# Letting the list scheduler choose between VectorE and GpSimd for SBUF-to-SBUF work, with a longer allowance for loads

## The chip, the cores and the metric

The kernel runs on one core of a Trainium2 chip. The metric is the device time of one execution in microseconds, the median of several runs. TensorE (PE) multiplies, VectorE (DVE), ScalarE (ACT) and GpSimd (POOL) do the elementwise work, and SyncE's queue (SP) issues nearly all DMAs.

## The reference

Three blocks follow each other. Windowed attention makes 1152 token rows of 512. A mixture of four experts (each 512 to 1024 to 512, ReLU) is added up with per-token weights. A last block goes 512 to 2048 to 512 with `h * cos(h)` between its two products:

```
x = attention(q, k, v)                        # 1152 x 512
p = domain_probs / (domain_probs.sum(-1, keepdims=True) + 1e-09)
for e in range(4):
    out += p[:, e:e + 1] * (np.maximum(x @ w1[e], 0.0) @ w2[e])
h = out @ w_in                                # w_in, w_out arrive as float64
result = (h * np.cos(h)) @ w_out
```

## The kernel before

Every fp32 product is made of three matmuls on rounded halves: an operand is split into a high part (`hi`, rounded by ACT) and a low part (`lo`, the rest, a subtraction), and PE adds hi*hi, hi*lo and lo*hi in PSUM. The feed-forward work is cut into steps of 512 hidden columns (two per expert, four for the last block), and a step into two units of 256. The tokens are cut into a group of 640 (two halves of 320) and one of 512 (two halves of 256).

The kernel has two parts. The first (attention, and expert 0 in its ordinary form) follows an order written out by hand, the string `ORDER`; it ends near 112 us. Everything after it is a list of jobs that `plan` (L1381) puts in order. From the third step on, the first product of a unit is a Strassen-Winograd scheme in seven products (`a_unit`, L988). It needs sums of token blocks (`tsum`, made in `t_jobs`, L915) and sums of weight blocks (`sums`, L823), each split into hi and lo again (`tlo`, `xlo`, `w7lo`). A unit's seven products depend on one another: DVE adds `y<-seed,p` (L1049) and `c<-seed,p` (L1058) between two of them, and PE waits for each. The second product of a unit (`b_unit`, L1205) needs 6 matmuls of 512 columns for every 128 tokens; `plan` puts these pieces between the dependent ones.

While the experts run, the float64 weights of the last block are converted on the side in 32 pieces (`conversion`, L706): DVE does five steps on each piece (`m` L724 and L730, `x` L740, L746 and L757), POOL one addition between the last two (`total`, L752), and the piece is stored to DRAM and loaded again later. Only when all 32 are stored may the last block's buffers be opened (`cos_ready`).

`plan` is a list scheduler. Each job has an engine, a duration and dependencies; jobs that read or write only SBUF on DVE, and all POOL jobs, share one resource called `port`, and two of them never run at once in the plan. Among the jobs that are ready on a free engine the one with the earliest due time (`late`) goes first. A load (SP) counts as landed 6.0 us after its issue, a conversion's load 4.5 us. The result is only an order for each engine. On the chip each engine runs its own list in that order and waits on semaphores, so nothing holds a POOL instruction back until the moment that the plan gave it. All weight sums and weight low parts, and the conversions' addition, are POOL's by hand; all token sums and low parts are DVE's.

Of the kernel before, what the change touches and what calls it, by code (L numbers as in the profile page):

```python
# [26 lines left out]
def tile_window_attention_moe_cosglu(  # L27
# [508 lines left out]
    class Job:  # L536
        __slots__ = ("eng", "ns", "fn", "deps", "new", "at", "late", "n", "out", "tail", "port")

# [10 lines left out]
    def job(eng, ns, fn, deps=(), new=(), use=(), tail=None, port=False):  # L549
        j = Job()  # L550
        j.tail = TAIL[eng] if tail is None else tail
        j.port = port or eng == "POOL"
        j.eng, j.ns, j.fn, j.new = eng, ns, fn, tuple(new)
# [152 lines left out]
    def conversion(i, half):  # L706
# [43 lines left out]

        def total():
            nc.gpsimd.tensor_tensor(  # L752
                out=box["x"], in0=box["x"], in1=box["m"].bitcast(F32), op=ALU.add
            )
# [55 lines left out]
    def w1_jobs(x, m):  # L810
# [12 lines left out]
        def sums(i):  # L823
            def fn():
# [8 lines left out]
                nc.gpsimd.tensor_tensor(out=o, in0=a, in1=b, op=op)  # L833
            return fn
# [20 lines left out]
        def low(i):  # L855
            def fn():
                nc.gpsimd.tensor_tensor(  # L857
                    out=operand(w_lo[x], i), in0=part(i),
                    in1=operand(w_hi[x], i).bitcast(F32), op=ALU.subtract,
                )  # L860
            return fn
# [4 lines left out]
        h1 = job("ACT", act_ns(256), high(1), [ld, h0], use=[hold])  # L866
        s0 = job("POOL", pool_ns(256), sums(0), [ld, h0], new=[hold_s], use=[hold])
        s1 = job("POOL", pool_ns(256), sums(1), [s0], use=[hold, hold_s])
        s2 = job("POOL", pool_ns(256), sums(2), [s0, s1], use=[hold, hold_s])
        h2 = job("ACT", act_ns(512), high(2), [s2, h0], use=[hold_s])  # L870
        s3 = job("POOL", pool_ns(256), sums(3), [s2], use=[hold, hold_s])
        h3 = job("ACT", act_ns(512), high(3), [s3, h0], use=[hold_s])
        w1_ready[x] = [
            job("POOL", pool_ns(size[i]), low(i), [h], use=[hold if i < 2 else hold_s])
            for i, h in enumerate((h0, h1, h2, h3))
        ]

    def w2_jobs(x, m):
        hold = Hold(raws)
        ld, box = load_job(x, hold)  # L880
        if m >= 3:
            war = list(w_users[first_kind[1][m - 3]])
        else:
            old = [(0, 0), (0, 1), (1, 0)][m]
            war = [
                std_b.get(s) for s, (e, g, f) in enumerate(steps)
                if (e, f // 2) == old and g == NG - 1
            ]
        before = [w_first[1, m - 1]] if m else []

        def high(i):
            def fn():
                if i == 0:
                    w_hi[x] = w2p.tile([P, 2, DM], F32R, tag="w2hi", name="whi")
                    w_lo[x] = w2p.tile([P, 2, DM], F32R, tag="w2lo", name="wlo")
                nc.scalar.copy(out=w_hi[x][:, i], in_=box["t"][:, i])  # L896
            return fn

        def low(i):
            def fn():  # L900
                nc.gpsimd.tensor_tensor(  # L901
                    out=w_lo[x][:, i], in0=box["t"][:, i], in1=w_hi[x][:, i].bitcast(F32),
                    op=ALU.subtract,
                )
# [10 lines left out]
    def t_jobs(k, deps_of, engines=("DVE", "DVE", "DVE"), own=False):  # L915
        n, ready = SN[k], []

        def columns(a, w):
            c1, c2 = slice(a, a + w), slice(n + a, n + a + w)
            k1, k2 = slice(0, 2), slice(2, 4)  # L920
            hold, box = Hold(tsums if own else raws), {}
            eng = engines[a // P]
            engine = nc.vector if eng == "DVE" else nc.gpsimd
            cost = dve_ns if eng == "DVE" else pool_ns

            def whole(o, ks, cs):
                def fn():
                    if o == 0:
# [11 lines left out]
            def less(o, i, j):  # L940
                def fn():
# [16 lines left out]
            def low(i):  # L958
                return lambda: nc.vector.tensor_tensor(  # L959
                    out=outs(xlo, tlo)[i], in0=ins()[i], in1=outs(xhi, thi)[i].bitcast(F32),  # L960
                    op=ALU.subtract,
                )

            j = None
            for fn in (
                whole(0, k1, c2), whole(1, k2, c2), less(2, 1, 0), whole(3, k1, c1),
                less(0, 0, 3), less(1, 1, 0), whole(3, k2, c1), less(3, 3, 1),
            ):
                j = job(
                    eng, cost(2 * w), fn, [j] if j else deps_of(a, w),  # L970
                    new=() if j else [hold], use=[hold] if j else (), port=True,
                )
            for i, m in enumerate((2 * w, 6 * w)):
                h = job("ACT", act_ns(m), high(i), [j], use=[hold])
                ready.append(job("DVE", dve_ns(m), low(i), [h], use=[hold], port=True))
        for a in range(0, n, P):
# [342 lines left out]
    for q, (c, k, u) in enumerate(order_units):  # L1319
# [3 lines left out]
        if c == NM and (c, k) not in x_ready:  # L1323
            n = SN[k]

            def deps_of(a, w, k=k, n=n):
# [5 lines left out]

            x_ready[c, k] = t_jobs(k, deps_of, ("DVE", "DVE", "DVE"), True) + [
                j for (kk, i, what), j in x_parts.items() if kk == k and what == "l"
# [41 lines left out]
    def gap(a, b):  # L1376
        if a.eng is None or b.eng is None:
            return 0.0
        return AGAIN[a.eng] if a.eng == b.eng and a.eng != "SP" else a.tail

    def plan(starts):  # L1381
# [44 lines left out]
        engines = ["PE", "ACT", "DVE", "POOL", "SP", None]  # L1426
        waiting = {e: [j for j in jobs if j.eng == e and not left[j]] for e in engines}
        busy = dict.fromkeys(engines, 0.0)
        began, events, now, done = {}, [(0.0, -1, None)], 0.0, 0
        seen, port = 0, 0.0  # L1430
        todo = list(pe_list)
        while events:
            now = events[0][0]
            while events and events[0][0] <= now + 1e-6:
# [8 lines left out]
                for o in j.out:  # L1443
                    left[o] -= 1
                    ready_at[o] = max(ready_at[o], now + gap(j, o))
                    if not left[o]:
                        waiting[o.eng].append(o)
                        if ready_at[o] > now:
                            seen += 1
                            heapq.heappush(events, (ready_at[o], seen, None))  # L1450
            for e in engines:
                while waiting[e] and busy[e] <= now + 1e-6:
                    ok = [
                        j for j in (todo[:AHEAD] if e == "PE" else waiting[e])
                        if not left[j] and not (j.port and port > now + 1e-6) and ready_at[j] <= now + 1e-6 and all(
                            free[h.slots] > (e == "SP" or e == "PE" and j is not todo[0])
                            for h in j.new
                        )
                    ]
# [3 lines left out]
                    waiting[e].remove(j)  # L1463
                    if e == "PE":
# [5 lines left out]
                    if j.port:  # L1470
                        port = busy[e]
                    seen += 1
# [18 lines left out]
    for j in sorted(jobs, key=lambda j: (began[j], rank[j])):  # L1491
        j.fn()
    lctx.close()
# [40 lines left out]
```

## Time and profile before

| what | value |
|---|---|
| median of 3 runs (lowest, highest) | 646.13 us (644.01, 646.4) |
| the profiled execution's own time | 645.96 us |
| its span, first to last instruction | 644.1 us |
| PE busy | 625.4 us (97%) |
| DVE busy | 447.9 us (70%), 864 instructions |
| ACT busy | 332.0 us (52%) |
| POOL busy | 313.1 us (49%), 302 instructions |
| mean granted TensorE clock | 0.994 of full speed |

1.9 us of the execution lie outside the span. PE is busy nearly throughout, so what can be saved without changing its work is the time in which it stands still or runs at the lower clock. DVE and POOL are averages over stages: between 176 and 432 us both are far busier than their shares say.

### The profile page before, as it was taken

The page shows a single profiled execution, that of the slowest core. Times are in us where ns is not written, and L with a number is a line of the kernel's source. Part 1 is how long each engine was busy: PE and PEld are TensorE (multiplying, and loading weights), DVE is VectorE, ACT ScalarE, POOL GpSimd, SP SyncE. Part 2 cuts the span into 40 slices and gives each one's busy share as a digit, 9 for nine tenths or more (in the row PEclk, how much of TensorE's full clock was granted, in tenths as well). Part 3 has the DMA queues.
Part 4 walks back from the last instruction along what each step waited for, and adds up shares of the span by engine and source line. Part 5 has one row for each costly group of instructions (what it writes and reads, how often), then busy time and mean ns, then how long its engine had stood idle before and what let it go on. Part 6 is the DMA issues. An engine that isn't in the chain of part 4 may idle for free.

```text
span 644.1 us, 10771 instructions
## 1 busy us (share of the span) xinstructions
PE 625.4 (97%) x4019; PEld 552.5 (86%) x4019; DVE 447.9 (70%) x864; ACT 332.0 (52%) x828; POOL 313.1 (49%) x302
## 2 busy tenths in 40 slices
PE   8999999999989999999999999999789999999997
PEld 7888898788879899989989888988588898999896
DVE  5767537226866878897777989888954565666664
ACT  5857413323243443353343443456678978767653
POOL 6984100912467387388477586445207426331000
PEclk9999999999989999999999999999899999999999
DMA  9943200340222635614445644301101202100012
GB/s 300 299 139 100 68 1 9 123 164 0 67 98 81 212 103 182 192 50 165 163 105 175 244 131 121 110 33 67 34 0 48 85 1 66 34 1 0 1 63 85
DMA packets 37253, 63.09 MB, mean 98 GB/s; under 512 B 2761, under 2 KB 18633, under 8 KB 37202
## 3 DMA queue, kind: packets, MB, share of 16 engines
q1 hardware_dynamic: 36386, 61.63, 30.1%
q10 hardware_dynamic: 816, 0.79, 0.4%
q8 instruction: 31, 0.51, 0.3%
q14 instruction: 20, 0.16, 0.1%
HBM read 51.66 MB, written 10.75 MB: 97 GB/s over the span
## 4 chain that ended last, share of the span: by engine, by line
PE 79%; DVE 11%; ACT 5%; issue 2%; DMA 2%; POOL 1%; SPq 0%; DVEq 0%; POOLq 0%
PE pb_acc L1205 32%; PE y L1018 17%; PE seed L1018 13%; PE pb_acc L465 7%; PE ph L617 3%; ACT e L281 1%; PE ph L428 1%; PE ph L429 1%; PE ph L430 1%; DVE tsum L943 1%; DMA raw<-in_moe_w_dram 1%; DVE tsum L934 1%; PE psv L321 1%; DVE acc L476 1%; DVE m L730 1%
## 5 line engine op out<-in xcount | busy, mean ns | idle before, releaser
L1205 PE MATMUL pb_acc<-whi,hh 128*128 128x512 f32 x360 | 142.7, 396 | 3.3 <-ACT hh L1146 3.3
L1205 PE MATMUL pb_acc<-wlo,hh 128*128 128x512 f32 x360 | 142.4, 396 | 0.0
L1205 PE MATMUL pb_acc<-whi,hl 128*128 128x512 f32 x360 | 141.1, 392 | 0.3 <-DVE hl L1152 0.3
L1018 PE MATMUL y<-xlo,w7hi 128*128 128x256 f32 (+1 forms) x320 | 95.0, 297 | 1.0 <-DVE xlo L959 0.9
L1018 PE MATMUL y<-xhi,w7hi 128*128 128x256 f32 (+1 forms) x320 | 95.1, 297 | 0.0
L1018 PE MATMUL y<-xhi,w7lo 128*128 128x256 f32 (+1 forms) x320 | 94.8, 296 | 0.0
L1205 PEld LDWEIGHTS pb_acc<-whi,hl 128*128 128x128 f32 x360 | 68.2, 189 | 16.3 <-DVE hl L1152 0.7
L901 POOL TENSOR_TENSOR wlo<-raw,whi 128x512 fp32r<-128x512 f32 x40 | 54.7, 1385 | 52.9 <-ACT whi L896 52.8
L1205 PEld LDWEIGHTS pb_acc<-whi,hh 128*128 128x128 f32 x360 | 68.3, 190 | 13.6 <-ACT hh L1146 3.7
L1018 PE MATMUL seed<-thi,w7hi 128*128 128x320 f32 (+1 forms) x240 | 72.5, 302 | 7.2 <-DVE c L1058 3.0
L752 POOL TENSOR_TENSOR x<-x,m 128x512 f32<-128x512 f32 x32 | 44.9, 1409 | 69.9 <-DVE x L746 64.5
L1205 PEld LDWEIGHTS pb_acc<-wlo,hh 128*128 128x128 f32 x360 | 68.3, 190 | 9.1
L857 POOL TENSOR_TENSOR w7lo<-raw,w7hi 128x512 fp32r<-128x512 f32 (+1 forms) x40 | 44.4, 1111 | 62.7 <-ACT w7hi L852 62.7
L1018 PE MATMUL seed<-thi,w7lo 128*128 128x320 f32 (+1 forms) x240 | 71.0, 296 | 0.0
L1018 PE MATMUL seed<-tlo,w7hi 128*128 128x320 f32 (+1 forms) x240 | 70.8, 295 | 0.0
L857 POOL TENSOR_TENSOR w7lo<-sums,w7hi 128x512 fp32r<-128x512 f32 x40 | 54.7, 1376 | 30.8 <-ACT w7hi L852 30.7
L1018 PEld LDWEIGHTS y<-xlo,w7hi 128*128 128x128 f32 x320 | 60.6, 189 | 3.3 <-DVE xlo L959 1.7
L1018 PEld LDWEIGHTS y<-xhi,w7hi 128*128 128x128 f32 x320 | 60.6, 189 | 2.2 <-DVE hl L1110 0.3
L1018 PEld LDWEIGHTS y<-xhi,w7lo 128*128 128x128 f32 x320 | 60.5, 189 | 0.0
L1018 PEld LDWEIGHTS seed<-thi,w7hi 128*128 128x128 f32 x240 | 45.2, 188 | 15.2 <-DVE c L1058 5.1
L476 DVE SCALAR_TENSOR_TENSOR acc<-pb_acc,gate_p,acc 128x512 f32<-128x512 f32 x63 | 45.9, 743 | 13.4 <-PE pb_acc L1205 13.3
L833 POOL TENSOR_TENSOR sums<-raw 128x256 f32<-128x256 f32 x40 | 34.2, 860 | 38.3 <-DVE xlo L959 37.7
(125 smaller groups left out, 1365.3 us busy)
## 6 DMA issues: line engine op xcount, KB each, us to landing
raw<-in_moe_w_dram SPq DMA_DIRECT2D x32, 512.0 KB, 5.2
raw<-in_moe_w_in_dram SPq DMA_DIRECT2D x16, 512.0 KB, 4.2
w<-x SPq DMA_DIRECT2D x32, 256.0 KB, 4.5
raw<-in_moe_w_out_dram SPq DMA_DIRECT2D x16, 512.0 KB, 4.1
raw<-w SPq DMA_DIRECT2D x16, 512.0 KB, 3.3
vr<-in_v_dram SPq DMA_DIRECT2D x16, 256.0 KB, 4.2
out_dram<-acc SPq DMA_DIRECT2D x18, 128.0 KB, 1.8
qraw<-in_q_dram SPq DMA_DIRECT2D x16, 128.0 KB, 3.7
```

The costliest lines, as they stand in the source:

```text
L281: nc.scalar.activation(out=e[:, p], in_=s[:, p], func=AF.Exp, bias=nm[:, p:p + 1], scale=1.0, accum_out=sm[:, p:p + 1],)
L321: nc.tensor.matmul(out=pv[W * h:W * (h + 1), p, W * c:W * (c + 1)], lhsT=vts[c][:, P * p + W * h:P * p + W * (h + 1)], rhs=pts[h][:, p, W ...
L428: nc.tensor.matmul(out=ps, lhsT=whi[:, d, cs], rhs=xh[:, d, :], start=d == 0, stop=False)
L465: nc.tensor.matmul(out=ps, lhsT=a, rhs=b, start=first and m == 0, stop=last and m == 2)
L476: nc.vector.scalar_tensor_tensor(out=a, in0=ps, scalar=p, in1=a, op0=ALU.mult, op1=ALU.add)
L617: nc.tensor.matmul(out=ps, lhsT=a[:, d, cs], rhs=b[:, d, :], start=d == 0 and m == 0, stop=d == KD - 1 and m == 2,)
L752: nc.gpsimd.tensor_tensor(out=box["x"], in0=box["x"], in1=box["m"].bitcast(F32), op=ALU.add)
L833: nc.gpsimd.tensor_tensor(out=o, in0=a, in1=b, op=op)
L857: nc.gpsimd.tensor_tensor(out=operand(w_lo[x], i), in0=part(i), in1=operand(w_hi[x], i).bitcast(F32), op=ALU.subtract,)
L901: nc.gpsimd.tensor_tensor(out=w_lo[x][:, i], in0=box["t"][:, i], in1=w_hi[x][:, i].bitcast(F32), op=ALU.subtract,)
L1018: nc.tensor.matmul(out=ps, lhsT=a[:, WI[i], d, :], rhs=b[:, d, :], start=start and d == 0 and m == 0, stop=d == 1 and m == 2, skip_group_c ...
L1205: nc.tensor.matmul(out=ps, lhsT=a[:, cs], rhs=b[:, fo, :], start=first and fo == 0 and m == 0, stop=last and fo == 1 and m == 2,)
```

## The change

Weight sums, weight low parts, token sums, token low parts and the conversions' addition become jobs made by `either`: they have a size instead of a fixed engine, stand in the waiting lists of both DVE and POOL, and whichever of the two `plan` finds free first takes the job, at that engine's cost (77 + 1.01 n ns on DVE, 147 + 2.16 n ns on POOL, n elements per partition). Three rules go with it. DVE doesn't take such a job if it is due more than 60 us later (`SOON`). POOL takes nothing while more than one port job is ready for DVE (`QUIET`). And the engine that did not hold the port last is asked first. `POOLMAX` (9999) excludes nothing. What waits for a load or a store is now planned 2.5 us later (`SPARE`).

```diff
+    def either(n, fn, deps=(), new=(), use=()):
+        j = job("POOL", pool_ns(n), fn, deps, new, use)
+        j.size = n
+        return j
...
+    SPARE = 2500.0
...
-        j = job("POOL", pool_ns(n), total, [j])
+        j = either(n, total, [j])
...
-        s0 = job("POOL", pool_ns(256), sums(0), [ld, h0], new=[hold_s], use=[hold])
+        s0 = either(256, sums(0), [ld, h0], new=[hold_s], use=[hold])
...
-            job("POOL", pool_ns(size[i]), low(i), [h], use=[hold if i < 2 else hold_s])
+            either(size[i], low(i), [h], use=[hold if i < 2 else hold_s])
...
-            job("POOL", pool_ns(DM), low(i), [h], use=[hold]) for i, h in enumerate((h0, h1))
+            either(DM, low(i), [h], use=[hold]) for i, h in enumerate((h0, h1))
...
-                j = job(
-                    eng, cost(2 * w), fn, [j] if j else deps_of(a, w),
-                    new=() if j else [hold], use=[hold] if j else (), port=True,
+                j = either(
+                    2 * w, fn, [j] if j else deps_of(a, w),
+                    new=() if j else [hold], use=[hold] if j else (),
                 )
...
-                ready.append(job("DVE", dve_ns(m), low(i), [h], use=[hold], port=True))
+                ready.append(either(m, low(i), [h], use=[hold]))
...
+    POOLMAX = 9999
+    QUIET = 1
+    SOON = 60000.0
...
-        return AGAIN[a.eng] if a.eng == b.eng and a.eng != "SP" else a.tail
+        if a.eng == "SP":
+            return a.tail + SPARE
+        return AGAIN[a.eng] if a.eng == b.eng else a.tail
...
+        def arrive(j):
+            for e in ("DVE", "POOL") if j.size else (j.eng,):
+                waiting[e].append(j)
...
-            for e in engines:
+            turn_of = {"DVE": ("POOL", "DVE"), "POOL": ("DVE", "POOL")}[owner]
+            for e in ("PE", "ACT", *turn_of, "SP", None):
                 while waiting[e] and busy[e] <= now + 1e-6:
                     ok = [
                         j for j in (todo[:AHEAD] if e == "PE" else waiting[e])
+                        if not (e == "DVE" and j.size and j.late > now + SOON)
+                        and not (e == "POOL" and j.size > POOLMAX)
...
+                    if e == "POOL" and sum(
+                        j.port and ready_at[j] <= now + 1e-6 for j in waiting["DVE"]
+                    ) > QUIET:
+                        break
...
+                    if j.size:
+                        j.eng, j.ns = e, (dve_ns if e == "DVE" else pool_ns)(j.size)
+                        j.tail = TAIL[e]
```

Counted over the whole program, 143 instructions go from POOL to DVE: 62 of the 80 `sums` (256 elements), 58 of the weights' low parts (2 of 256 elements, 56 of 512) and 23 of the 32 additions of the conversions (512). Four of `t_jobs` go from DVE to POOL. PE, ACT and SP issue what they issued before, in a changed order for PE from the unit that stood near 313 us on.

The first place is DVE in the first two units of the group of 512 tokens after the experts' Strassen form begins (176 to 190 us in the trace before). Line numbers are those of each file; `y_2251` before and `y_2242` after is the same addition, the one that the unit's next product waits for. Before:

```order
L730 SCALAR_TENSOR_TENSOR m_2212<-raw_2156,m_2212 128x512
L724 TENSOR_SCALAR m_2270<-raw_2182 128x512
L740 TENSOR_SCALAR x_2213<-m_2212 128x512
L730 SCALAR_TENSOR_TENSOR m_2270<-raw_2182,m_2270 128x512
L746 SCALAR_TENSOR_TENSOR x_2213<-raw_2156,x_2213 128x512
L740 TENSOR_SCALAR x_2271<-m_2270 128x512
L1049 TENSOR_TENSOR y_2251<-seed,p_2273 128x256
```

And after:

```order
L840 TENSOR_TENSOR sums<-raw 128x256
L864 TENSOR_TENSOR w7lo<-raw,w7hi 128x512
L840 TENSOR_TENSOR sums<-raw 128x256
L764 SCALAR_TENSOR_TENSOR x_2071<-raw_1986,x_2071 128x512
L840 TENSOR_TENSOR sums<-raw,sums 128x256
L476 SCALAR_TENSOR_TENSOR acc<-pb_acc,gate_p,acc 128x512
L1053 TENSOR_TENSOR y_2242<-seed,p_2264 128x256
```

The weight sums that POOL made beside this stretch stand on DVE itself now, and the third and fourth conversion pieces have moved behind it.

The second place is DVE in a unit near 390 us, from its `y<-seed,p` on. Before:

```order
L1049 TENSOR_TENSOR y_4374<-seed,p_4394 128x256
L730 SCALAR_TENSOR_TENSOR m_4389<-raw_4319,m_4389 128x512
L757 SCALAR_TENSOR_TENSOR x_4309<-raw_4239,x_4309 128x512
L740 TENSOR_SCALAR x_4390<-m_4389 128x512
L1110 SCALAR_TENSOR_TENSOR hl<-y_4362,hh 128x256
L476 SCALAR_TENSOR_TENSOR acc<-pb_acc,gate_p,acc 128x512
L1058 TENSOR_TENSOR c_4443<-seed,p_4394 128x256
```

And after, the same unit from the same addition:

```order
L1053 TENSOR_TENSOR y_4378<-seed,p_4397 128x256
L753 SCALAR_TENSOR_TENSOR x_4389<-raw_4289,x_4389 128x512
L476 SCALAR_TENSOR_TENSOR acc<-pb_acc,gate_p,acc 128x512
L759 TENSOR_TENSOR x_4389<-x_4389,m_4388 128x512
L1114 SCALAR_TENSOR_TENSOR hl<-y_4365,hh 128x256
L764 SCALAR_TENSOR_TENSOR x_4389<-raw_4289,x_4389 128x512
L1062 TENSOR_TENSOR c_4446<-seed,p_4397 128x256
```

The conversion's addition (L759) stands between DVE's own steps, so its last step (L764) no longer follows on POOL.

The third place is the change from the experts to the last block (432 to 470 us). On DVE, from the low parts of the first token group's sums to the first unit's `y<-seed,p`, stood before:

```order
L959 TENSOR_TENSOR tlo<-tsum,thi 128x6x128
L959 TENSOR_TENSOR xlo<-tsum,xhi 128x2x128
L959 TENSOR_TENSOR tlo<-tsum,thi 128x6x128
L959 TENSOR_TENSOR xlo<-tsum,xhi 128x2x128
L476 SCALAR_TENSOR_TENSOR acc<-pb_acc,gate_p,acc 128x512 x3
L1049 TENSOR_TENSOR y_4916<-seed,p_4931 128x256
```

And after:

```order
L963 TENSOR_TENSOR xlo<-tsum,xhi 128x2x128 x2
L1114 SCALAR_TENSOR_TENSOR hl<-seed,hh 128x320
L908 TENSOR_TENSOR wlo<-raw,whi 128x512
L476 SCALAR_TENSOR_TENSOR acc<-pb_acc,gate_p,acc 128x512
L908 TENSOR_TENSOR wlo<-raw,whi 128x512
L840 TENSOR_TENSOR sums<-raw 128x256
L864 TENSOR_TENSOR w7lo<-raw,w7hi 128x512
L1053 TENSOR_TENSOR y_4899<-seed,p_4916 128x256
```

Four weight jobs now stand among the steps ahead of that addition (a fifth, `sums`, follows right behind it). On POOL, beside the token sums of the second group, stands after:

```order
L864 TENSOR_TENSOR w7lo<-sums,w7hi 128x512 x2
L938 TENSOR_TENSOR tsum<-xhi,xlo 128x128
L947 TENSOR_TENSOR tsum<-tsum 128x128
L908 TENSOR_TENSOR wlo<-raw,whi 128x512 x2
L963 TENSOR_TENSOR xlo<-tsum,xhi 128x2x128
```

The `w7lo` and `wlo` stood on POOL before as well; the two `tsum` and the `xlo` are new to it.

## Rows read from the trace of the kernel before

**Rows 1.** Windows: stretch, length, busy us (instructions) by engine, granted clock, DMA.
```profile
core 0: us, PE busy (x) PEld busy (x) DVE busy (x) ACT busy (x) POOL busy (x), PEclk, DMA share, GB/s
112.00:176.00 64.00, 63.91 (x323) 54.66 (x322) 34.09 (x67) 19.95 (x40) 30.50 (x30) 1.00 0.28 88
176.00:432.00 256.00, 251.36 (x1469) 224.92 (x1469) 206.38 (x343) 103.08 (x233) 167.77 (x142) 0.99 0.43 137
268.99:312.87 43.88, 43.79 (x268) 39.06 (x267) 36.03 (x62) 18.03 (x42) 28.82 (x24) 1.00 0.44 143
363.27:411.11 47.84, 46.14 (x280) 40.60 (x279) 42.07 (x65) 18.29 (x43) 33.13 (x27) 1.00 0.45 148
432.00:496.00 64.00, 56.90 (x323) 49.29 (x322) 48.20 (x104) 46.79 (x108) 24.26 (x24) 0.97 0.10 34
```

**Rows 2.** Waits of PE: who waited for whom, us in total, times, longest.
```profile
PE pb_acc L1205 <- ACT hh L1146: 3.3, 1, 3.3
PE seed L1018 <- DVE c L1058: 3.0, 4, 1.2
PE seed L1018 <- DVE y L1049: 2.2, 1, 2.2
PE seed L1018 <- ACT seed L1032: 1.9, 3, 1.2
```

**Rows 3.** Timeline of PE, 186 to 191 us: start, length, what, wait before.
```profile
186.18 0.43 PE L1018 MATMUL seed<-thi,w7hi 128*128 128x256 f32 x1 [2.21 <-DVE y L1049]
...
188.75 0.63 PE L1205 MATMUL pb_acc<-whi,hh 128*128 128x512 f32 x1
...
190.61 0.28 PE L1018 MATMUL seed<-thi,w7hi 128*128 128x256 f32 x1
```

**Rows 4.** The chain that ended last: start, length, merged matmuls.
```profile
287.63 1.42 PE y L1018 x12
289.06 1.39 PE pb_acc L1205 x6
```

**Rows 5.** Timeline of PE, 461 to 467 us.
```profile
461.47 0.50 PE L1205 MATMUL pb_acc<-whi,hh 128*128 128x512 f32 x1 [3.31 <-ACT hh L1146]
...
466.49 0.39 PE L1205 MATMUL pb_acc<-whi,hh 128*128 128x512 f32 x1
```

**Rows 6.** Line 757: durations in ns (min/median/max), first and last start.
```profile
L757 DVE SCALAR_TENSOR_TENSOR x<-raw,x x32: 677/1188/1787, 170.3 to 408.8; 128x512 f32<-128x512 f32 x32
```

**Rows 7.** Timeline of DVE, 368 to 370 us.
```profile
368.23 0.68 DVE L746 SCALAR_TENSOR_TENSOR x<-raw,x 128x512 f32<-128x512 uint32 x1
368.83 0.74 DVE L476 SCALAR_TENSOR_TENSOR acc<-pb_acc,gate_p,acc 128x512 f32<-128x512 f32 x1
369.49 0.41 DVE L1110 SCALAR_TENSOR_TENSOR hl<-seed,hh 128x256 fp32r<-128x256 f32 x1
369.82 0.75 DVE L724 TENSOR_SCALAR m<-raw 128x512 uint32<-128x512 uint32 x1
```

**Rows 8.** Groups of POOL's instructions by shape: busy us, mean ns, idle before.
```profile
L752 POOL TENSOR_TENSOR x<-x,m 128x512 f32<-128x512 f32 x32 | 44.9, 1409 | 69.9 <-DVE x L746 64.5 <-PE seed L1018 2.8 <-PE y L1018 2.6
```

**Rows 9.** Timeline of DVE, 449 to 470 us.
```profile
449.22 1.38 DVE L934 TENSOR_TENSOR tsum<-xhi,xlo 128x128 f32<-128x128 f32 x1
...
451.78 0.28 DVE L934 TENSOR_TENSOR tsum<-xhi,xlo 128x128 f32<-128x128 f32 x1
...
454.98 1.52 DVE L934 TENSOR_TENSOR tsum<-xhi,xlo 128x256 f32<-128x256 f32 x1
...
469.12 0.42 DVE L959 TENSOR_TENSOR xlo<-tsum,xhi 128x256 fp32r<-128x256 f32 x1
```

**Rows 10.** Timeline of POOL, 448 to 457 us.
```profile
448.99 1.46 POOL L857 TENSOR_TENSOR w7lo<-sums,w7hi 128x512 fp32r<-128x512 f32 x1 [4.17 <-ACT w7hi L852]
453.63 2.59 POOL L901 TENSOR_TENSOR wlo<-raw,whi 128x512 fp32r<-128x512 f32 x2 [3.19 <-ACT whi L896]
```

More of the change, by code (lines that the diff above doesn't have):

```diff
@@ L536, in tile_window_attention_moe_cosglu @@
     class Job:
-        __slots__ = ("eng", "ns", "fn", "deps", "new", "at", "late", "n", "out", "tail", "port")
+        __slots__ = ("eng", "ns", "fn", "deps", "new", "at", "late", "n", "out", "tail", "port", "size")
     jobs = []
@@ L552, in job @@
         j.port = port or eng == "POOL"
+        j.size = 0
         j.eng, j.ns, j.fn, j.new = eng, ns, fn, tuple(new)
@@ L749, in low, with total @@
             )
-        def total():
-            nc.gpsimd.tensor_tensor(
+        def total(engine):
+            engine.tensor_tensor(
                 out=box["x"], in0=box["x"], in1=box["m"].bitcast(F32), op=ALU.add
@@ L823, in sums, with fn @@
         def sums(i):
-            def fn():
+            def fn(engine):
                 if i == 0:
@@ L832, in fn @@
                 )[i]
-                nc.gpsimd.tensor_tensor(out=o, in0=a, in1=b, op=op)
+                engine.tensor_tensor(out=o, in0=a, in1=b, op=op)
             return fn
@@ L855, in low, with fn @@
         def low(i):
-            def fn():
-                nc.gpsimd.tensor_tensor(
+            def fn(engine):
+                engine.tensor_tensor(
                     out=operand(w_lo[x], i), in0=part(i),
@@ L910, in w2_jobs, with t_jobs @@
         w2_ready[x] = [
-            job("POOL", pool_ns(DM), low(i), [h], use=[hold]) for i, h in enumerate((h0, h1))
+            either(DM, low(i), [h], use=[hold]) for i, h in enumerate((h0, h1))
         ]
-    def t_jobs(k, deps_of, engines=("DVE", "DVE", "DVE"), own=False):
+    def t_jobs(k, deps_of, own=False):
         n, ready = SN[k], []
@@ L921, in columns, with fn @@
             hold, box = Hold(tsums if own else raws), {}
-            eng = engines[a // P]
-            engine = nc.vector if eng == "DVE" else nc.gpsimd
-            cost = dve_ns if eng == "DVE" else pool_ns
             def whole(o, ks, cs):
-                def fn():
+                def fn(engine):
                     if o == 0:
@@ L940, in less, with fn @@
             def less(o, i, j):
-                def fn():
+                def fn(engine):
                     t = box["t"]
@@ L1426, in plan @@
         engines = ["PE", "ACT", "DVE", "POOL", "SP", None]
-        waiting = {e: [j for j in jobs if j.eng == e and not left[j]] for e in engines}
+        waiting = {e: [] for e in engines}
+        def arrive(j):
+            for e in ("DVE", "POOL") if j.size else (j.eng,):
+                waiting[e].append(j)
+        for j in jobs:
+            if not left[j]:
+                arrive(j)
         busy = dict.fromkeys(engines, 0.0)
         began, events, now, done = {}, [(0.0, -1, None)], 0.0, 0
-        seen, port = 0, 0.0
+        seen, port, owner = 0, 0.0, "POOL"
         todo = list(pe_list)
@@ L1454, in plan @@
                         j for j in (todo[:AHEAD] if e == "PE" else waiting[e])
-                        if not left[j] and not (j.port and port > now + 1e-6) and ready_at[j] <= now + 1e-6 and all(
+                        if not (e == "DVE" and j.size and j.late > now + SOON)
+                        and not (e == "POOL" and j.size > POOLMAX)
+                        and not left[j] and not (j.port and port > now + 1e-6) and ready_at[j] <= now + 1e-6 and all(
                             free[h.slots] > (e == "SP" or e == "PE" and j is not todo[0])
@@ L1462, in plan @@
                     j = ok[0] if e == "PE" else min(ok, key=lambda j: (j.late, j.n))
-                    waiting[e].remove(j)
+                    for x in ("DVE", "POOL") if j.size else (e,):
+                        waiting[x].remove(j)
+                    if j.size:
+                        j.eng, j.ns = e, (dve_ns if e == "DVE" else pool_ns)(j.size)
+                        j.tail = TAIL[e]
                     if e == "PE":
@@ L1470, in plan @@
                     if j.port:
-                        port = busy[e]
+                        port, owner = busy[e], e
                     seen += 1
@@ L1491, in tile_window_attention_moe_cosglu @@
     for j in sorted(jobs, key=lambda j: (began[j], rank[j])):
-        j.fn()
+        if j.size:
+            j.fn(nc.vector if j.eng == "DVE" else nc.gpsimd)
+        else:
+            j.fn()
     lctx.close()
```

16 lines of the change are left out of this document (8 added, 8 removed).

## The prediction

> **What bounds the kernel now.** I read the windows of busy time first. Between 112 and 176 us PE is busy 63.91 of 64.00 us, between 176 and 432 us 251.36 of 256.00, between 432 and 496 us 56.90 of 64.00 [rows 1]. So PE bounds nearly everything, and after the part that is ordered by hand it stands still in two places: 4.6 us among the conversions and 7.1 us at the change to the last block. The waits of PE come next: in those stretches they are waits for DVE's two additions between dependent products, for ACT's seed copy, and one of 3.3 us for ACT's `hh` [rows 2]. The timeline then shows what a stop costs on top of itself. After the 2.21 us wait at 186.18 us six 512-column matmuls take 1.86 us (188.75 to 190.61) [rows 3], where six take 1.39 elsewhere [rows 4]; the twelve 256-column ones ahead of them take 2.57 us (186.18 to 188.75) [rows 3] instead of 1.42 [rows 4]. [...] After the 3.31 us wait twelve 512-column matmuls reach from 461.47 to 466.49 us [rows 5], 5.02 instead of 2 x 1.39 = 2.78; less a 0.30 us wait within, that is 1.9 us. All that a better order could win behind 112 us is thus 0.1 + 4.6 + 7.1 + 1.6 + 1.9 = 15.3 us. PE's matmuls themselves are not changed.
>
> Then why DVE is late. The line that follows POOL's conversion addition takes 0.677 us at best, 1.188 in the median and 1.787 at worst [rows 6]. The same happens to token sums: 1.38 us for 128 columns and 1.52 for 256, against 0.28 undisturbed [rows 9] and 0.41 for a 256-column instruction [rows 7]. Both stand beside POOL instructions that began just before, at 448.99 and 453.63 us [rows 10]. A DVE instruction that reads SBUF stands behind a running POOL instruction for most of that instruction's time, up to 1.787 - 0.677 = 1.1 us.
>
> [...]
>
> **The change part by part.** First the engines' load. Successive starts on DVE lie 0.60 us apart for 512 columns from SBUF, 0.66 for 512 from PSUM, 0.33 for 256 [rows 7]; the same 512-column addition takes POOL 1.409 us [rows 8]. Moved are 64 instructions of 256 columns and 79 of 512: 64 x 0.33 + 79 x 0.60 = 68.5 us more for DVE, some 50 of them (61 of 512 and 38 of 256) in the units that stand between 175 and 439 us. With the lengths of these starts, DVE's own instructions of those 22 units sum to 164 us before and 214 us after. The window of 176 to 432 us has DVE busy 206.38 us [rows 1], so some 42 us of it is time behind the 142 POOL instructions there, 0.30 us for each. About 49 POOL instructions remain in these units, so DVE after is about 214 + 49 x 0.30 = 229 us against 264 us of time. Its load rises from 81% to some 87%, while POOL's hold on the port falls to a third. Neither engine is then the bound over the whole stretch; what counts is the single places.
>
> [...]
>
> Place one, 172 to 191 us: waits of 0.6 and 2.2 us, and 1.6 us of clock, 4.4 us together. There DVE's conversion steps stood behind POOL's weight sums and low parts, one after another, and the addition that PE needed came behind all of them. After, the sums stand on DVE at 0.33 us each, the next conversion steps come later, and POOL has half as many instructions beside them. What is left in front of the addition is 3 x 0.33 + 2 x 0.60 + 0.66 = 2.9 us of DVE work, which PE covers with products and fill work. I take 80% of it: -3.6 us. Bounds: -4.4, and +1 if the four accumulator additions and sums ahead of the first unit's addition make PE wait in their turn.
>
> Place two, 363 to 411 us: 1.7 us of waits (47.84 less 46.14) [rows 1]. DVE's instructions for these four units sum to 29.5 us before and 40.3 after; busy it was 42.07 [rows 1], so 12.6 us went behind 27 POOL instructions, 0.47 each. After, about ten remain: 40.3 + 4.7 = 45.0 us, of 46.1 that PE needs. DVE is fuller than before, with fewer long blocks. I take no gain: 0, bounds -1.7 and +3.
>
> Place three, 432 to 496 us: 7.1 us of waits and 1.9 us of clock. Here a chain bounds: last accumulator tile, transposes, token sums, low parts, first product, with DVE at work all through it until 469.12 + 0.42 us [rows 9]. On that way DVE lost 1.10 + 1.11 us in the two instructions shown, and some 1 us in two smaller ones. After, the two `wlo` still stand on POOL there (1.3 us each by [rows 10]), and two token sums and an `xlo` are new on POOL, which takes twice as long for them; but the fill work of PE is spread between the transposes. Ahead of the chain DVE gets five weight jobs, 3 x 0.60 + 2 x 0.33 = 2.5 us, in place of POOL instructions that blocked it for about 2 us. I take a quarter: -2.3 us; bounds -9.0 and +3.
>
> The other moved instructions (21 after 470 us, 23 before 175 us) lie on a DVE with room: 34.09 of 64.00 us busy between 112 and 176 us [rows 1]. Cost 0; without that cover they would cost their 0.33 to 0.60 us each. The longer allowance only puts loads' users later in the plan; PE waits for no load in these stretches [rows 2], so 0, bounds -0.5 and +2 (a raw tile held longer). Fuller DVE elsewhere: +0.5, bounds 0 and +4.
>
> Sum: -3.6 + 0 - 2.3 + 0 + 0.5 = -5.4 us against the profiled execution's 645.96 us (span 644.1 plus 1.9 outside), which is the median 646.13 within 0.2. Forecast **640.5 us**.
>
> **Rivals.** *DVE becomes the bound among the conversions.* Place: 363 to 411 us (spare 46.1 - 40.3 = 5.8 us for ten POOL instructions) and the four units of 269 to 313 us (37.3 us of DVE work in a window of 43.88 [rows 1], for eight). It decides once a remaining POOL instruction costs DVE 0.6 to 0.8 us instead of 0.47. At the worst seen, 1.1 us, the first is 5.2 us late and the second 2.2, and two single units whose own DVE work (13.5 and 13.0 us) fills the time of 3.5 x 1.78 + 5 x 1.39 = 13.2 us (1.78 us for twelve 320-column matmuls, scaled from [rows 4] by columns) lose 2 us each: 11.4 us, and three stops of the kind at 186 us add 3 x 1.6 us of clock. With only place one gained: 646 + 16.2 - 3.6 = 658.6; at 0.8 us about 652. I take 654. For it: before, one place in that stretch had such a shortage already. Against: DVE and POOL together ask less of the port than before.
>
> *The chain moves nothing.* Place three stays as it is, since a chain of latencies doesn't ask who made the weights, and its five added jobs eat half of place one: 646 - 3.6 + 2.5 = 645, no change.
>
> *All waits go.* The places with DVE behind POOL lose both their waits and their clock, and only the 1.2 us for the seed copy and half the chain remain: 645.96 - 15.3 + 1.2 + 2 = 634.
>
> *The change doesn't do what it says:* the order shows 143 moved instructions, so this is out.
>
> **How the numbers follow.** Forecast 0.45 (its own range 636.5 to 642.8), all waits gone 0.13, chain unmoved 0.23, DVE as the bound 0.19. A measurement of this kernel can tell about 0.5%, 3.2 us, from no change. Faster 0.45 + 0.13 = 0.58, same 0.23, slower 0.19. The range of 632 to 652 us takes in the gain's end and DVE's shortage at 0.8 us, and leaves some 0.05 below and 0.12 above.
>
> **What would show it.** Right: DVE busy about 490 to 505 us and POOL about 150 to 165; line 764 (757 before) with a median under 0.9 us; no wait of PE over 1 us between 172 and 200 us, and full clock there; a wait of 2 to 3 us left at the change to the last block. Wrong: new waits of PE for `y` or `c` between 230 and 420 us that sum to over 5 us (the bound has moved to DVE), or a wait in the chain over 4 us (place three is worse). A granted clock under 0.99 would point to either.

## Result, and the profile after

| | median of runs (lowest to highest) | before, on the same chip | ratio, 95% interval |
|---|---|---|---|
| changed kernel | 648.13 us (647.57 to 653.45, 9 runs) | 645.85 us | 1.0056 [1.0037, 1.0075] |
| changed kernel, second time | 647.40 us (645.72 to 652.08, 12 runs) | 645.90 us | 1.0033 [1.0015, 1.0050] |

By the medians the change costs 1.5 to 2.3 us, where 5.4 us of gain were forecast. It is on the wrong side of zero in both series; of the two ratios, 0.56% and 0.33%, only the second lies inside the 0.5% that the forecast called no change. The first profiled run of the changed kernel was its slowest and had lost 5.5 us before the planned part began, in instructions whose order the change doesn't touch; the second began that part at 101.78 us against 101.76 before, so the rows below are of the second (in its files lines 764, 1022, 1053 and 1209 are what 757, 1018, 1049 and 1205 were before).

Its engines' busy time first, from the page's part 1:

```profile
span 644.9 us, 10784 instructions
PE 626.3 (97%) x4019; PEld 552.3 (86%) x4019; DVE 491.1 (76%) x1003; ACT 334.1 (52%) x828; POOL 157.8 (24%) x163
```

The windows that answer to [rows 1], with the same columns:

```profile
112.00:176.00 64.00, 60.62 (x287) 51.26 (x287) 39.62 (x78) 18.69 (x37) 7.32 (x6) 0.97 0.23 75
176.00:432.00 256.00, 252.00 (x1490) 225.98 (x1489) 230.70 (x448) 104.77 (x231) 55.51 (x46) 1.00 0.44 140
432.00:496.00 64.00, 59.65 (x338) 51.57 (x337) 53.34 (x117) 48.16 (x112) 16.36 (x17) 0.97 0.10 34
```

DVE and POOL came out as forecast: 491.1 and 157.8 us in all, and DVE 230.70 us among the conversions (229 was forecast). But the first window has turned over. Before, PE was busy 63.91 of its 64 us at full clock [rows 1]; now it is 60.62 at a granted clock of 0.97. The forecast had called this stretch the one with room on DVE.

What PE waited for, in place of [rows 2]:

```profile
PE pb_acc L465 <- DVE acc L476: 3.4, 1, 3.4
PE seed L1022 <- DVE c L1062: 3.2, 4, 2.1
...
PE pb_acc L1209 <- ACT hh L1150: 1.3, 1, 1.3
PE seed L1022 <- DVE y L1053: 1.1, 3, 0.4
```

The 2.2 us wait for `y` and the 3.3 us wait for `hh` are gone or small. New are a single wait of 3.4 us for `acc`, which no row of before has, and one of 2.1 us for `c`. The timeline of PE at the first (start, length, what, wait before):

```profile
113.44 0.40 PE L465 MATMUL pb_acc<-whi,hl 128*128 128x512 f32 x1
117.21 0.51 PE L465 MATMUL pb_acc<-whi,hh 128*128 128x512 f32 x1 [3.38 <-DVE acc L476]
...
118.25 0.63 PE L465 MATMUL pb_acc<-wlo,hh 128*128 128x512 f32 x1
...
121.66 0.39 PE L465 MATMUL pb_acc<-whi,hh 128*128 128x512 f32 x1
```

From 117.21 to 121.66 us stand twelve 512-column matmuls: 4.45 us, where twelve take 2 x 1.39 = 2.78 [rows 4]. The granted clock over them is 0.62 of full speed (in the first run too, over the same twelve, and 0.50 from 123.69 to 126.68 us). So the stop took 3.38 us itself and 1.67 more at the lower clock, 5.1 us in all. What DVE did meanwhile:

```profile
107.78 0.74 DVE L476 SCALAR_TENSOR_TENSOR acc<-pb_acc,gate_p,acc 128x512 f32<-128x512 f32 x1
...
111.24 0.84 DVE L840 TENSOR_TENSOR sums<-raw 128x256 f32<-128x256 f32 x1
...
112.61 0.41 DVE L840 TENSOR_TENSOR sums<-raw 128x256 f32<-128x256 f32 x1
112.94 0.68 DVE L864 TENSOR_TENSOR w7lo<-raw,w7hi 128x512 fp32r<-128x512 f32 x1
113.54 0.41 DVE L840 TENSOR_TENSOR sums<-raw,sums 128x256 f32<-128x256 f32 x1
...
114.68 0.68 DVE L442 SCALAR_TENSOR_TENSOR hl<-ph,hh 128x512 fp32r<-128x512 f32 x1
115.28 0.28 DVE L963 TENSOR_TENSOR xlo<-tsum,xhi 128x128 fp32r<-128x128 f32 x1
115.48 0.68 DVE L864 TENSOR_TENSOR w7lo<-sums,w7hi 128x512 fp32r<-128x512 f32 x1
116.08 0.41 DVE L840 TENSOR_TENSOR sums<-raw,sums 128x256 f32<-128x256 f32 x1
116.42 1.40 DVE L476 SCALAR_TENSOR_TENSOR acc<-pb_acc,gate_p,acc 128x512 f32<-128x512 f32 x2
```

And in the kernel before:

```profile
112.21 2.06 DVE L476 SCALAR_TENSOR_TENSOR acc<-pb_acc,gate_p,acc 128x512 f32<-128x512 f32 x3
```

Before, the three additions (line 476) that empty an expert step's PSUM tiles ran together. After, the first runs at 107.78 us and the other two 8.6 us later, behind six moved weight operations (four `sums`, two `w7lo`), an `hl` and token lows. PE needs their PSUM buffers: the next step's four accumulators come out of a pool of four. The planner doesn't know this. It gives an accumulator a buffer reservation (`Hold`) in `std_bs`, but this step's tiles were opened in the hand-ordered part, so `std_hold` has no entry for them. In the planner's own table the two additions are due at 78.5 and 318.4 us of the planned part, and the matmuls that need the buffers stand at 12.2. In the kernel before they were due some 60 us behind these matmuls too, but nothing with an earlier due time was ready for DVE there, so they ran in time by accident.

Where the time went, by PE's starts of the same instructions. A "seed group" is an unbroken run of `seed` matmuls; there are 121.

| start, us | before | changed | e1 | e6 |
|---|---|---|---|---|
| first planned `ph` | 101.76 | 101.78 | 101.68 | 101.80 |
| first `y` product | 134.84 | 139.94 | 134.57 | 134.69 |
| 14th seed group | 195.51 | 196.53 | 191.15 | 191.26 |
| 58th seed group | 367.89 | 372.20 | 366.81 | 365.52 |
| 69th seed group | 412.09 | 414.70 | 409.32 | 408.02 |
| 92nd seed group | 518.25 | 518.60 | 512.85 | 511.56 |
| last matmul | 640.05 | 640.80 | 635.06 | 633.76 |

Changed less before, stretch by stretch: +5.08, -4.08, +3.29, -1.70, -2.26, +0.40 us, together with the 0.02 at the start 0.75. (e1 and e6 are the experiments below.)

### The profile page after: what moved, and what is told of

The parts are those of the page before. It is cut to its first block, busy times and chain, and to the rows that moved or that the text cites. A ratio compares the mean times of both kernels' runs of the same rounds, so it can differ in the third digit from the quotient of the medians.

```text
span 651.6 us, 10784 instructions
## 1 busy us (share of the span) xinstructions
PE 630.3 (97%) x4019; PEld 556.5 (85%) x4019; DVE 493.1 (76%) x1003; ACT 334.7 (51%) x828; POOL 156.7 (24%) x163
## 4 chain that ended last, share of the span: by engine, by line
PE 41%; DVE 17%; ACT 6%; issue 2%; DVEq 0%; ACTq 0%
PE pb_acc L1209 21%; PE y L1022 11%; PE seed L1022 9%; DVE m L737 1%; ACT kk L1142 1%; DVE sums L840 1%; DVE hl L1114 1%; DVE acc L476 1%; DVE x L753 1%; ACT kk L1141 1%; DVE tsum L938 1%; DVE x L759 1%; DVE x L764 1%; DVE tsum L947 1%; ACT kk L1130 1%
## 5 line engine op out<-in xcount | busy, mean ns | idle before, releaser
L864 POOL TENSOR_TENSOR w7lo<-raw,w7hi 128x256 fp32r<-128x256 f32 (+1 forms) x25 | 25.6, 1034 | 160.2 <-ACT w7hi L859 160.2
L1022 PEld LDWEIGHTS seed<-tlo,w7hi 128*128 128x128 f32 x240 | 45.1, 188 | 3.5
L908 POOL TENSOR_TENSOR wlo<-raw,whi 128x512 fp32r<-128x512 f32 x17 | 24.0, 1419 | 89.3 <-ACT whi L903 77.3
L1022 PEld LDWEIGHTS seed<-thi,w7lo 128*128 128x128 f32 x240 | 45.1, 188 | 0.0
L439 ACT ACTIVATE hh<-y 128x320 fp32r<-128x320 f32 (+1 forms) x48 | 19.6, 408 | 46.3 <-PE y L1022 46.3
```

The source lines that it names most:

```text
L439: nc.scalar.activation(out=hh, in_=ps, func=AF.Relu)
L864: engine.tensor_tensor(out=operand(w_lo[x], i), in0=part(i), in1=operand(w_hi[x], i).bitcast(F32), op=ALU.subtract,)
L908: engine.tensor_tensor(out=w_lo[x][:, i], in0=box["t"][:, i], in1=w_hi[x][:, i].bitcast(F32), op=ALU.subtract,)
L1022: nc.tensor.matmul(out=ps, lhsT=a[:, WI[i], d, :], rhs=b[:, d, :], start=start and d == 0 and m == 0, stop=d == 1 and m == 2, skip_group_c ...
```

## Experiments

Theory A: the loss is the wait for the two additions, which the list puts behind work with an earlier due time. Rival B: it is the fuller DVE among the conversions.

**e1: the additions early.** Only the two additions move, to where the first one stands.

```diff
+            if not hold:
+                script_adds.append(std_done[k, c + i])
...
+    early_adds = sorted((j for j in script_adds), key=lambda j: began[j])
+    for i, j in enumerate(early_adds):
+        began[j] = began[early_adds[0]] + 0.01 * i
```

> The changed kernel with one edit: the three additions of the last hand-started expert step (acc L476) are issued one behind another on DVE, as in the kernel before; everything else keeps its place. Theory A (the loss is the 3.4 us wait of pb_acc at 122.7 us for these additions, and the nine matmuls at the lower clock behind it): the wait goes, 5 us less than the changed kernel's 648.1, so 643 us, 2 to 3 us under the kernel before. Rival B (the loss is the fuller DVE among the conversions between 176 and 432 us): nothing changes there, 648 us, and the wait's time comes back at a later wait.

641.73 us (640.65 to 645.46, 7 runs) against 645.46 for the kernel before: 0.9950 [0.9929, 0.9971]. In e1's trace the three additions stand together again, and its first window is full:

```profile
107.68 2.07 DVE L476 SCALAR_TENSOR_TENSOR acc<-pb_acc,gate_p,acc 128x512 f32<-128x512 f32 x3
```
```profile
112.00:176.00 64.00, 63.59 (x323) 54.77 (x322) 44.85 (x89) 21.43 (x44) 8.33 (x7) 1.00 0.24 75
```

DVE does more work in this window than in the changed kernel (44.85 against 39.62 us), and PE waits for it once, 0.41 us at 174.97 us. By the table the last matmul comes 5.74 us earlier than in the changed kernel, and nothing is given back later. Theory A holds, B falls: two instructions, moved, turn the loss into a gain of 3.7 us.

**e2: the additions late in the kernel before.** The reverse: eight passes over a tile ahead of the second addition.

```diff
+    std_done, REPEAT = {}, 8
...
+                if not std_hold.get((e, g)) and i == 1:
+                    for _ in range(REPEAT):
+                        a = acc[k][:, c + i, :]
+                        nc.vector.tensor_scalar(out=a, in0=a, scalar1=1.0, scalar2=None, op0=ALU.mult)
```

> The kernel before with one edit: between the first and the second of the three additions (acc L476) DVE runs eight more passes over a 128x512 tile (multiplied by 1.0), in a stretch where DVE is idle for 6 us right after. Theory A: pb_acc at 113 us waits for the passes, some 2.5 to 5 us, and then runs at the lower clock for some matmuls: 649 to 652 us. Rival B (it is the conversions that pay): the 3 to 5 us of DVE work fall into DVE's idle time, 646 us, as before.

655.31 us (655.12 to 656.08, 4 runs): 1.0153 [1.0139, 1.0168], 9.9 us slower. DVE, PE and one row of POOL, at the place:

```profile
113.02 8.07 DVE L662 TENSOR_SCALAR acc<-acc 128x512 f32<-128x512 f32 x8
121.13 1.41 DVE L476 SCALAR_TENSOR_TENSOR acc<-pb_acc,gate_p,acc 128x512 f32<-128x512 f32 x2
```
```profile
121.93 0.80 PE L465 MATMUL pb_acc<-whi,hh 128*128 128x512 f32 x1 [7.79 <-DVE acc L476]
```
```profile
117.10 2.85 POOL L861 TENSOR_TENSOR w7lo<-sums,w7hi 128x512 fp32r<-128x512 f32 x2
```

My size was off: a pass took 1.01 us and not 0.3 to 0.6. POOL's weight work ran beside all eight: seven POOL instructions follow each other from 113.63 to 120.77 us, 1.02 us apart. The mechanism is as said: 8.07 us of DVE work made 7.79 us of wait, though DVE had time right behind it.

**e3: the allowance undone.** The changed kernel, planned anew.

```diff
-    SPARE = 2500.0
+    SPARE = 0.0
```

> The changed kernel with the longer allowance for loads alone undone (0 in place of 2500 ns; the plan is made anew, and puts the three additions at 14.6 to 15.8 us, all behind the weights' work). Theory A: the wait at 122 us stays, at 3.4 us or more, 648 us or a little over. If the allowance were what costs: 643 to 645 us, with no wait over 1 us there.

650.02 us (645.96 to 651.53, 8 runs): 1.0061 [1.0039, 1.0084]. The wait stays and is longer (theory A):

```profile
PE pb_acc L465 <- DVE acc L476: 3.9, 1, 3.9
```

As far as this run goes, the allowance isn't what costs here. But the order that this plan makes computes a wrong result, for a reason that isn't known, so its time is weaker evidence than the others'.

**e5: the planner is told.** The first matmuls of the next expert step depend on the additions; all else is planned anew.

```diff
         if f == 0:
             std_hold[e, g] = [Hold(accs) for _ in range(no)]
+            deps += script_adds
+            script_adds.clear()
...
+            if not hold:
+                script_adds.append(std_done[k, c + i])
```

> The changed kernel with one rule more for the planner: the first matmuls of an expert step whose four buffers are freed by the hand-started additions depend on these additions, so that they get an early due time; the plan is made anew. Theory A: the additions stand at 7.3 to 8.5 us of the plan, no wait at 122 us, 643 us, give or take 2 us for the waits that another order brings. Rival B: 648 us.

643.00 us (641.84 to 644.69, 5 runs) against 645.46: 0.9953 [0.9939, 0.9968]. One missing dependency is the difference between a loss and a gain.

**after_again: the changed kernel once more.**

> The changed kernel itself once more, beside the others. Theory A: 648 us, with the wait of pb_acc for acc at about 17 us behind the start of the planned part, and the nine slow matmuls behind it. The 5.5 us that its first profiled run had lost before the planned part begins (107.3 against 101.8 us) belong to that run: here the planned part starts between 101.5 and 103.5 us. If they belonged to the change, it starts at 107 us again.

647.40 us, start of the planned part 101.78 us, the wait of 3.38 us in its place. Both points as expected.

**e6: one `c` ahead.** The second new wait is of the same kind. In the changed kernel DVE runs ten steps of two conversion pieces, due earlier, between an `hl` at 328.16 us and the `c` for which PE waits (the first `m` stands beside POOL's work):

```profile
326.70 1.54 DVE L731 TENSOR_SCALAR m<-raw 128x512 uint32<-128x512 uint32 x1
...
329.87 0.42 DVE L731 TENSOR_SCALAR m<-raw 128x512 uint32<-128x512 uint32 x1
...
333.88 0.68 DVE L759 TENSOR_TENSOR x<-x,m 128x512 f32<-128x512 f32 x1
334.49 0.49 DVE L1062 TENSOR_TENSOR c<-seed,p 128x320 f32<-128x320 f32 x1
```

e6 is e1 with this `c` issued five places earlier.

```diff
+    ahead = next(j for j in jobs if j.n == 929)
+    began[ahead] = began[next(j for j in jobs if j.n == 230)] - 0.01
```

> e1_adds_early with one more instruction moved: the c (line 1062 of the changed kernel) for which PE waits 2.1 us at 329.6 us is issued five places earlier on DVE, ahead of the last five of a row of conversion steps. Theory A (each wait of PE for an instruction that the list puts behind work with an earlier due time is lost whole): no wait over 0.6 us there, 2 to 3 us less than e1_adds_early, 639 us. Rival C (the conversion steps are the limit there, so that a later wait takes its place): 641.7 us as e1_adds_early, with a new wait of 1 to 2 us before 365 us.

639.35 us (638.50 to 639.90, 6 runs) against 645.90: 0.9901 [0.9884, 0.9918]. PE's waits for `c` in e6, all four:

```profile
PE seed L1024 <- DVE c L1064: 1.7, 4, 0.6
```

The 2.1 us wait is gone, the largest left is 0.6, and no new one over 0.6 follows: against the kernel before, the stretch between the 14th and the 58th group costs +1.88 us in place of e1's +3.28. The profiled runs differ by 1.3 us and the medians by 2.4, so the size is somewhere between. The clock may be part of it, which isn't shown: three of e1's seven runs have a granted clock of 0.994 or 0.995, and none of e6's six is under 0.997. DVE had the capacity; the order was at fault, and rival C falls.

**e7, e12: PSUM readers first.** Beside e5's dependency, DVE's readers of PSUM count as due 12 us earlier when the planner picks.

```diff
-                    j = ok[0] if e == "PE" else min(ok, key=lambda j: (j.late, j.n))
+                    j = ok[0] if e == "PE" else min(
+                        ok, key=lambda j: (j.late - (FIRST if e == "DVE" and not j.port else 0.0), j.n)
+                    )
```

> e5_planner_knows with one rule more: DVE's instructions that read PSUM (y, c, hl, acc) count as due 12 us earlier when the planner picks DVE's next one. Theory A: no wait over 1 us for y, c or acc between 110 and 440 us, 639 to 641 us. Rival C: the conversions and the weights come later, PE waits for weights or the converted words, 643 us or more.

640.79 us (640.49 to 643.25, 6 runs): 0.9932 [0.9914, 0.9951]. As expected no wait over 1 us before 440 us, but the rule put the last block's token sums behind DVE's readers of PSUM:

```profile
PE y L1026 <- ACT xhi L964: 6.0, 1, 6.0
```

e12 ends the rule at 320 us of the plan.

```diff
+    FIRST, UNTIL = 12000.0, 320000.0
...
-                        ok, key=lambda j: (j.late - (FIRST if e == "DVE" and not j.port else 0.0), j.n)
+                        ok, key=lambda j: (j.late - (FIRST if e == "DVE" and not j.port and now < UNTIL else 0.0), j.n)
```

> e7_evictions_first with its second rule (PSUM readers count as due 12 us earlier on DVE) only up to 320 us of the planned part, so that the token sums of the last block are not put behind them. Theory A: the gain of 8 us up to 440 us stays, the 6.0 us wait of y for xhi at 458 us falls to 1 to 3 us: 636 to 639 us. Rival C: the wait is the conversions' and stays: 641 us.

639.51 us (638.78 to 640.43, 6 runs): 0.9892 [0.9857, 0.9927]. The 6.0 us wait is gone; the longest behind it is 1.7. It ends 0.5 us above the expected range. With e6 it is the fastest version, some 1% under the kernel before.

**e4, e9, e10, e11: which edit brings the gain?** e4 gives the kernel before the longer allowance alone, e9 is e5 with all weights' jobs on POOL, e10 is e5 without POOL's rest, and e11 is the kernel before with e5's dependency (its diff is e5's).

```diff
e4: +        if a.eng == "SP":
    +            return a.tail + 2500.0
e9: -        j = either(n, total, [j])
    +        j = on_pool(n, total, [j])          # and so for sums and lows of the weights
e10:-    QUIET = 1
    +    QUIET = 9999
```

> The kernel before with the longer allowance for loads alone (2500 ns more); engines as before. The forecast put the allowance at 0: 646 us. Rival D (the allowance brings part of the gain by earlier weights): 643 us or less. Rival E (with all weights on POOL the earlier due times of the weights push the token sums and conversions back): waits of PE of 7 us near 171 us and of 4 to 6 us between 430 and 465 us, 655 to 665 us.

> e5_planner_knows with the weights' operations (totals, sums, lows) given to POOL as in the kernel before; the token sums' choice, the longer allowance and the early additions stay. If the weights that left POOL bring the gain (forecast places one and three): the 2.2 us wait for y at about 186 us and the waits before the last block are back, 645 to 647 us. If the allowance or the token sums bring it: 643 us or less.

> e5_planner_knows without the rule that POOL begins nothing while two or more of DVE's SBUF-to-SBUF operations are ready: the free choice then gives POOL 247 operations again in place of 90 (the plan made anew). If the gain is POOL's rest from SBUF work, the waits before 440 us come back and the time is that of the kernel before or worse, 646 to 660 us; if the choice by itself brings it: 643 us.

> The kernel before with the one rule of e5_planner_knows (the four buffers' additions before the next expert step), engines and allowance as before. There was no wait at this place in the kernel before, so by theory A nothing is gained: 646 us. If the rule by itself were a gain, 643 us.

| | median | ratio to before, 95% interval | PE's longest waits for `xhi` |
|---|---|---|---|
| e4 | 658.91 us | 1.0192 [1.0151, 1.0232] | 5.6 us at 178, 6.8 at 450 |
| e9 | 666.21 us | 1.0320 [1.0300, 1.0340] | 25.1 us at 459 |
| e10 | 649.60 us | 1.0051 [1.0028, 1.0074] | 8.5 us at 442 |
| e11 | 645.39 us | 0.9983 [0.9961, 1.0005] | none |

PE's waits of e4, of e9 and of e10:

```profile
PE y L1018 <- ACT xhi L956: 13.4, 3, 6.8
PE pb_acc L1205 <- ACT hh L1146: 2.4, 1, 2.4
```
```profile
PE y L1029 <- ACT xhi L967: 25.1, 1, 25.1
```
```profile
PE y L1026 <- ACT xhi L964: 8.5, 1, 8.5
```

e4 went as rival E said: the allowance alone makes the weights due earlier, and on a kernel whose weights are all POOL's the token sums fall behind. e9 missed, and e10's time lay in its first range for another reason than the one given. I had expected the 2.2 us wait at 186 us back in e9 and the waits before 440 us back in e10. They are gone in both, and both lose at the change to the last block instead. e9's PE is even fuller than e1's between 176 and 432 us:

```profile
176.00:432.00 256.00, 255.59 (x1505) 229.92 (x1504) 191.99 (x321) 105.38 (x235) 167.43 (x145) 1.00 0.41 132
```

So the waits among the conversions can be planned away with POOL as busy as before (167.43 against 167.77 us [rows 1]). The 69th seed group starts at 404.16 us in e9 and at 404.15 in e10, 7.9 us earlier than in the kernel before and 3.9 earlier than in e6: up to there the orders with more POOL work are the best of all. What these three kernels, all with the longer allowance and over 230 us planned for POOL, lose is the last block: its `xhi` come 7 to 25 us late, and in none of the kernels with the weights mostly on DVE more than 6.0. That POOL's share together with the allowance is the reason is argued from this comparison; the kernel before has POOL as busy without the allowance, and no such wait. Which rule clears the place at 186 us isn't settled: the choice without the allowance (e3), without POOL's rest (e10), and with the weights left on POOL (e9) all clear it, and the allowance without the choice (e4) leaves 0.9 us of it. e11 shows that the dependency is worth nothing where nothing stands ahead of the additions.

## Why the prediction was wrong

**The step that failed** is "The other moved instructions (21 after 470 us, 23 before 175 us) lie on a DVE with room: 34.09 of 64.00 us busy between 112 and 176 us. Cost 0". The 23 before 175 us cost 5.08 us, all in one wait and the clock behind it (e1, e2); the 21 after 470 us brought no new wait of PE (the 1.2 us for ACT's seed copy at 481 us stood there before). The room was real, and e1 uses it: DVE is busier there and PE waits 0.4 us in all. But an average share over 64 us says nothing about who stands behind a moved instruction in an in-order list. Here these were two additions on which PE's next accumulators depended, with a due time so late that anything went ahead of them. The price in the same sentence, "their 0.33 to 0.60 us each" without cover, counted DVE time. Six such operations are 4 x 0.33 + 2 x 0.60 = 2.5 us (the first took 0.4 more than that); with the `hl` and the token low that now stand ahead too (0.8 us) and the 1.67 us of lower clock behind the stop they make up about the 5.1. The forecast did name accumulator additions, at place one some 60 us later and with a bound of +1. None of the four rivals held this case.

**Place one** (172 to 191 us, forecast -3.6): -4.08 us up to the 14th seed group, and -4.09 in e1. No wait over 1 us is left there. The size held, in part by luck: the 1.6 us of clock in the forecast came from the one trace of the kernel before (1.86 - 1.39 and 2.57 - 1.42 us by [rows 3] and [rows 4], at a granted clock of 0.61 from 186.18 to 190.61 us). e11's trace has the same wait (2.26 us) with matmuls of 0.28 us from the second behind it on, where before has 0.41, and takes 59.22 us from the first `y` product to the 14th group, where before took 60.67 and the changed kernel 56.59. Against e11 the gain is 2.6 us. That the weights' leaving POOL is what does it isn't shown, since e9 gets the same with the weights on POOL.

**Fuller DVE elsewhere** (+0.5, bounds 0 and +4) was mis-sized: +3.29 us between the 14th and the 58th group, of which e6 takes back 1.4 by moving one instruction. In e6 three waits of PE of 0.4 to 0.6 us and one of 0.2 are left there. In the first run of the changed kernel, where the clock fell behind the wait for `c`, the same stretch cost 4.84.

**Place two** (363 to 411 us, forecast 0): -1.70, the lower bound. The rival that DVE becomes the bound there is out: POOL was busy 4.86 us in that window of the changed kernel, where I had left ten instructions:

```profile
363.27:411.11 47.84, 47.31 (x292) 42.24 (x291) 42.46 (x88) 19.32 (x44) 4.86 (x4) 1.00 0.44 135
```

**Place three** (432 to 496 us, forecast -2.3): -2.26 us from the 69th to the 92nd group, -2.63 in e1. The forecast's 1.9 us of clock stood at a granted clock of 0.66, from 461.47 to 466.49 us before. The wait for `hh` fell from 3.3 to 1.3 us, and a chain of shorter waits stayed, as said.

**The allowance** (0): in the changed kernel undoing it gains nothing (e3, with its reserve). Alone it costs 12.6 us (e4), so the 0 holds only beside the free choice; the reason I gave, that PE waits for no load, was the wrong question, since due times move every other job.

**Line 764** has the median forecast (under 0.9 us), in place of [rows 6]:

```profile
L764 DVE SCALAR_TENSOR_TENSOR x<-raw,x x32: 675/680/1782, 180.5 to 406.6; 128x512 f32<-128x512 f32 x32
```

Without the one wait the change is a gain, as forecast, but a smaller one: e1's median is 3.7 us under the kernel before (641.73 us, where 640.5 were forecast). Its trace looks better, with the last matmul 4.99 us earlier than before, in part because before's trace lost 1.6 us of clock at place one, which e11's didn't. Two errors also cancel in part (+3.29 for +0.5, -1.70 for 0).

## What to carry to other kernels

When work is added to an in-order engine, list what stands behind it and who waits for that; spare time over a window was no cover here (DVE was busy 39.62 of 64 us, and PE waited 3.38 us for two additions of DVE's). Where a planner sets the order, look for resources that it doesn't know (here PSUM buffers opened before its part began): such a job gets a due time that means nothing, and goes well only as long as its engine is idle. Take a stop's price with the clock behind it, and as a range where the clock differs from run to run (0 or 1.6 us behind the same wait of 2.1).

## What the runs showed of the hardware

A stop's length alone doesn't say whether the clock falls behind it. The same stop, in two runs of the same kernel, did both. In the second run of the changed kernel the 2.08 us wait is followed by matmuls at full clock (granted 1.00 from 335.03 to 340 us),

```profile
335.03 0.42 PE L1022 MATMUL seed<-thi,w7hi 128*128 128x320 f32 x1 [2.08 <-DVE c L1062]
335.28 0.31 PE L1022 MATMUL seed<-tlo,w7hi 128*128 128x320 f32 x1
```

and in its first run, with the same instructions ahead of it, the clock falls 1.2 us behind the wait (granted 0.69 from 340.54 to 346 us):

```profile
340.54 0.42 PE L1022 MATMUL seed<-thi,w7hi 128*128 128x320 f32 x1 [2.07 <-DVE c L1062]
...
342.16 0.63 PE L1209 MATMUL pb_acc<-whi,hl 128*128 128x512 f32 x1
```

From the end of the wait to the last of the next twelve `y` matmuls it is 3.97 us in the second run and 5.53 in the first, so the fall cost 1.6. Likewise the 2.21 us wait of the kernel before cost 1.6 us of clock [rows 3] (granted 0.61), and a wait of 2.26 us at the same place in e11 nothing:

```profile
187.62 0.39 PE L1022 MATMUL seed<-thi,w7hi 128*128 128x256 f32 x1 [2.26 <-DVE y L1053]
187.85 0.28 PE L1022 MATMUL seed<-tlo,w7hi 128*128 128x256 f32 x1
```

What decides between the two isn't shown. After 3.38 us it was 1.67 us, and after e2's 7.79 some 3.1, an estimate: its first `y` product stood 11.01 us later than before, 0.16 of it at the start of the planned part and 7.79 the wait. The 512-column matmuls right behind that wait took 0.63 us, the two ahead of it 0.40.

Some DVE instructions beside POOL took about as long as POOL's. e2's eight passes took 1.01 us each beside POOL instructions 1.02 us apart; no run shows the same pass without POOL. In the second run of the changed kernel `m` of the same shape took 1.54 us beside the first of these two POOL instructions (1.37 us each), and 0.42 when they had ended, 3 us later on the same engine (326.70 and 329.87 above):

```profile
326.66 2.74 POOL L864 TENSOR_TENSOR w7lo<-sums,w7hi 128x512 fp32r<-128x512 f32 x2
```

What DVE waits for there isn't shown; the `port` is a resource of the plan.
